# Decode attention with a gated MLP on one core: other places for the rows of wo, and most of w2 loaded in mid-run

## The chip, the core and the metric

The kernel runs on one core of a Trainium2 chip. The metric is the device time of one execution in microseconds (us). The core has a matrix engine (TensorE, PE; its weight loads are PEld), a vector engine (VectorE, DVE), a scalar engine (ScalarE, ACT), GpSimd (POOL) and SyncE (SP), which here only issues transfers. Transfers run on 16 DMA engines, numbered 0 to 15 in this text.

## The reference

One token attends over 32 heads with a cache of 4096 positions each, and the result is mixed with a small MLP of the same token:

```
g = sigmoid(sum(x * gate_w))
q = x @ wq                              # 512 -> 32 heads x 128
p = softmax(q . k_cache / sqrt(128))    # 32 heads x 4096 positions
a = (p @ v_cache) @ wo                  # 32 x 128 -> 512
b = relu(x @ w1 + b1)**2 @ w2 + b2      # 512 -> 1376 -> 512
out = g * a + (1 - g) * b
```

All inputs are bfloat16. K and V are 32 MB each; wq and wo 4 MB each; w1 and w2 1.4 MB each.

## The kernel before

**Heads.** SP loads K and V head by head, 1 MB each, [128 partitions x 8 KB], into eight slots of Kt and eight of Vt; `load_k` and `load_v` wait until a slot is free. V of head h is issued with K of head h + LAG (7). In iteration i of the loop that PE, DVE and ACT each run, half of the scores of head i come from DVE (`ttr`, 16 fused multiply-and-sum instructions, line 636), the other half from PE: `transposes` (line 439) turns K, ACT copies the result out of PSUM, `scores` (line 450) multiplies by q. Maxima are taken for four heads at once (`max_rows`, `max_cols`), ACT makes the exponentials, and `pv` (line 475) multiplies head i - 7 by V, 32 matmuls. `den` and `norm` divide, eight heads at a time.

**wo.** W holds wq (4 MB) first. When q is complete (s_qps reaches 8), the rows of wo for heads 0 to 23 take its place: 96 rows of 32 KB, here called pieces, one to a partition of W. `place` gives the partition of a piece from its kind (INNER, OUTER, SEAM, WRAP) and an engine e; a run (kind, e, k, r, m) is one load of k x m pieces, meant for k DMA engines in a row from engine e on, m pieces each. POOL issues RUNS in the order of the list (line 330); where the next run starts on another engine than the last one ended on, a small load of d rows of w1 into `dm` (line 327) goes ahead, to move POOL's cursor by d engines. SP issues FIRST (line 278), three pieces each, one each in heads HF = 20 onwards, and last the piece REST (line 281). STRIPS lists all of it in order; POOL makes one selection a strip (line 345) for `selA`, the matrix with which `spread_a` (line 507) brings the normed results of heads 0 to 23 to the partitions in which their pieces lie. `out_a` (line 519) multiplies 23 of the 32 columns of W on PE in iterations 34 to 38; DVE does the other nine (`part_y`, lines 683 and 686), and `sum_y` (line 546) adds them in iteration 37. Both wait for all pieces (s_wp, s_wr).

**The MLP.** SP loads w1 at head 8; `mlp_h` (line 493) runs in iteration 24, DVE makes `hs` in iteration 25.

**The tail.** After the last V, when head 24 has left slot 0 of Kt, SP loads w2 in three parts (w2b, the last 96 rows; w2a, ten groups of 128 rows in two halves, split at GS) and the rows of wo for heads 24 to 31 into slot 0 of Kt, in two parts (`wob_sb`, 768 and 256 KB). Then it issues 15 loads of 16 bytes a row, with 1, 2, ... 15 rows (line 301), into a part of w1's tile that nothing reads after; it waits for them at the very end. PE runs `regroup` (lines 525 and 528: transposes the last eight heads and spreads them), then `mlp_out(0)`, `(1)` and `(2)` (line 555, four matmuls a group of rows), then `out_b` (line 537), all into the accumulator `acc`, whose first matmul is the one of `out_a` with start=True. DVE adds b2, PE transposes, DVE copies, SP stores 1 KB (line 303).

Of the kernel before, what the change touches and what calls it, by code (L numbers as in the profile page):

```python
# [5 lines left out]
def bass_gated_mix__gqa_block_cached__dense_activation_squared_relu__decode_kernel(  # L6
# [31 lines left out]
    F = 1376  # L38
    FG = 10
# [13 lines left out]
    LAG = 7  # L53
    NA = 24
    TB = 8
    GS = [0, 5, 10]
    TS = [0, 6, 8]
    TD = 23
    INNER, OUTER, SEAM, WRAP = range(4)
    RUNS = [(INNER, 0, 4, 0, 1), (INNER, 4, 12, 0, 2), (INNER, 4, 12, 1, 2),  # L60
            (OUTER, 4, 3, 0, 1), (SEAM, 7, 2, 0, 1), (OUTER, 9, 7, 0, 1),
            (OUTER, 4, 3, 1, 1), (SEAM, 7, 2, 1, 1), (OUTER, 14, 2, 1, 1),
            (SEAM, 7, 2, 2, 1), (WRAP, 15, 2, 3, 1), (SEAM, 7, 2, 3, 1)]
    FIRST = [(INNER, 0, 3, 1, 1), (INNER, 0, 3, 2, 1), (INNER, 0, 3, 3, 1),
             (OUTER, 0, 3, 0, 1), (OUTER, 0, 3, 1, 1), (OUTER, 0, 3, 2, 1)]
    REST = 126
    HF = 20

    def place(kind, e, k, r, m):
# [16 lines left out]
    def strips():  # L86
        q = 0
        for run in RUNS + FIRST:
            yield (*place(*run), q)
            q += place(*run)[2]  # L90
        yield REST, 1, 1, q

    STRIPS = list(strips())

# [3 lines left out]
    woa_v = A_wo.rearrange("(p t) n -> p (t n)", t=32)  # L98
    wob_v = A_wo[NA * 128:NH * 128, :].rearrange("(p t) n -> p (t n)", t=TB)
    w1_v = B_w1.rearrange("(p t) n -> p t n", t=4)  # L100
    w2_v = B_w2[0:FG * 128, :].rearrange("(p g) n -> p g n", g=FG)

    ctx = ExitStack()
    with ctx:
# [6 lines left out]
        def sem(name):  # L111
            return ctx.enter_context(nc.semaphore(name))
# [3 lines left out]
        W = sb("W", [128, 4 * 4096], bf16)  # L116
# [5 lines left out]
        w1_sb = sb("w1_sb", [128, 4, F], bf16)  # L122
# [121 lines left out]
        s_acc = sem("s_acc")  # L244
        s_fin = sem("s_fin")
        s_out = sem("s_out")
        s_pr = [sem(f"s_pr{n}") for n in range(15)]

        block = ctx.enter_context(nc.Block())

# [1 line left out]
        @block.sync  # L252
        def _(eng):
            for t in range(4):
                eng.dma_start(wq_sb[:, t, :], wq_v[:, t, :]).then_inc(s_wq[t], 16)  # L255

            def load_k(h):
                if h >= NK:
                    eng.wait_ge(s_sd, h - NK + 1)
                    eng.wait_ge(s_t, 2 * (h - NK + 1))  # L260
                eng.dma_start(Kt[:, h % NK, :], k_h[h, :, :]).then_inc(s_k[h % NK], 16)  # L261

            def load_v(h):
                if h >= NV:
                    eng.wait_ge(s_pv, h - NV + 1)
                eng.dma_start(Vt[:, h % NV, :], v_h[h, :, :]).then_inc(s_v[h % NV], 16)  # L266

            for h in range(LAG):
                load_k(h)
            for h in range(NH):  # L270
                load_v(h)
                if h + LAG < NH:
                    load_k(h + LAG)
                if h == HF:
                    eng.wait_ge(s_qps, 8)
                if HF <= h < HF + len(FIRST):
                    p, st, k, q = STRIPS[len(RUNS) + h - HF]
                    eng.dma_start(W[p:p + st * (k - 1) + 1:st, :], woa_v[q:q + k, :],
                                  max_dma_last_dim=8192).then_inc(s_wr, 16)
                if h == HF + len(FIRST):  # L280
                    eng.dma_start(W[REST:REST + 1, :].rearrange("p (s n) -> p s n", s=16),
                                  woa_v[4 * NA - 1:4 * NA, :].rearrange("p (s n) -> p s n", s=16))\
                       .then_inc(s_wr, 16)
                if h == 8:
                    eng.wait_ge(s_z, 1)
                    eng.wait_ge(s_b2, 1)
                    for t in range(4):
                        eng.dma_start(w1_sb[:, t, :], w1_v[:, t, :]).then_inc(s_w1, 16)
            eng.wait_ge(s_sd, NA + 1)
            eng.wait_ge(s_t, 2 * (NA + 1))  # L290
            eng.dma_start(w2b[:, :], B_w2[FG * 128:F, :]).then_inc(s_w2[0], 16)
            for c in range(len(GS) - 1):
                eng.dma_start(w2a[:, GS[c]:GS[c + 1], :], w2_v[:, GS[c]:GS[c + 1], :])\  # L293
                   .then_inc(s_w2[c + 1], 16)
            for c in range(len(TS) - 1):
                eng.dma_start(wob_sb[:, TS[c]:TS[c + 1], :],
                              wob_v[:, TS[c] * DM:TS[c + 1] * DM].rearrange("p (t n) -> p t n", n=DM))\
                   .then_inc(s_wo[c], 16)
            eng.wait_ge(s_sb, 1)
            for n in range(1, 16):  # L300
                eng.dma_start(w1_sb[0:n, 3, 32 * n:32 * n + 8], B_w1[0:n, 0:8]).then_inc(s_pr[n - 1], 16)
            eng.wait_ge(s_f4, 1)
            eng.dma_start(out[0, 0, :].rearrange("(j p) -> j p", p=128), fin4[:, :]).then_inc(s_out, 16)
            eng.wait_ge(s_out, 16)
            for q in s_pr:
                eng.wait_ge(q, 16)


        @block.gpsimd
# [89 lines left out]
        def _(eng):  # L399
# [111 lines left out]
            def out_a(n):  # L511
                if n == 0:
                    eng.wait_ge(s_ac, 2)
                    for q in s_wp:
                        eng.wait_ge(q, 16)
                    eng.wait_ge(s_wr, 16 * (len(FIRST) + 1))
                for t in range(4 * n, min(4 * n + 4, TD)):
                    for j in range(4):
                        eng.matmul(acc[:, j:j + 1], wo_sb[:, t, j * 128:(j + 1) * 128],
                                   o2A[:, t:t + 1], start=(t == 0 and j == 0), stop=False,  # L520
                                   skip_group_check=True)

            def regroup():
                eng.wait_ge(s_on, NH // HPO)
                eng.transpose(KP[0][0:NH - NA, 0:128], onorm[:, NA:NH], ident[:, :]).then_inc(s_oT, 1)
                eng.wait_ge(s_oc, 1)
                for c in range(16):
                    mm = eng.matmul(O2B, selB[:, c // 8, c % 8, :], oB[:, TB * c:TB * c + TB],
                                    start=(c == 0), stop=(c == 15))
                mm.then_inc(s_oT, 1)  # L530
# [17 lines left out]

            def mlp_out(c):
                eng.wait_ge(s_w2[c], 16)  # L550
                for n in [FG] if c == 0 else range(GS[c - 1], GS[c]):
                    M = 128 if n < FG else FR
                    w = w2a[:, n, :] if n < FG else w2b[:, :]
                    for j in range(4):
                        eng.matmul(acc[:, j:j + 1], w[:, j * 128:(j + 1) * 128], hs[0:M, n:n + 1],
                                   start=False, stop=False, skip_group_check=True)

            q_rows(0)
            q_cols(0)
# [3 lines left out]
            for i in range(NH + LAG):  # L563
                if i < NH:
                    transposes(i)
                if 1 <= i <= NH:
                    scores(i - 1)
                if i % 3 == 0 and i // 3 + 1 < 8:
                    q_rows(i // 3 + 1)
                if i % 3 == 2 and i // 3 + 1 < 8:  # L570
                    q_cols(i // 3 + 1)
                if i >= 5 and (i - 5) % 4 == 0 and (i - 5) // 4 < NG:
                    max_rows((i - 5) // 4)
                if i >= 6 and (i - 6) % 4 == 0 and (i - 6) // 4 < NG:
                    max_cols((i - 6) // 4)
                if i == 34:
                    out_a(0)
                if 34 <= i < 39:
                    out_a(i - 33)
                if i >= LAG:  # L580
                    pv(i - LAG)
                if i >= 12 and (i - 12) % HPO == 0:
                    den((i - 12) // HPO)
                if i == 24:
                    mlp_h()
                if i == 32:
                    turn_a()
                if i == 33:
                    spread_a()
                if i == 37:  # L590
                    sum_y()
            regroup()
            eng.wait_ge(s_hs, 2)
            for c in range(len(GS)):
                mlp_out(c)
            for c in range(len(TS) - 1):
                out_b(c)
            eng.wait_ge(s_fin, 1)
# [4 lines left out]
        def _(eng):  # L603
# [85 lines left out]
            for i in range(NH + LAG):  # L689
# [17 lines left out]
                if i == 33:  # L707
                    eng.wait_ge(s_at, 2)
                    eng.tensor_copy(o2A[:, :], O2A).then_inc(s_ac, 1)
                    eng.wait_ge(s_e, NS * 2)  # L710
                    eng.tensor_copy(o2D, O2A[:, TD:32]).then_inc(s_y2, 1)
                    for q in s_wp:
                        eng.wait_ge(q, 16)
                    eng.wait_ge(s_wr, 16 * (len(FIRST) + 1))
                    eng.wait_ge(s_y2, 1)
                    part_y()
            norm(NH // HPO - 1)
# [37 lines left out]
```

## Time and profile before

| | us |
|---|---|
| median of 3 runs | 199.5 (199.47 to 199.66) |
| the profiled execution | 199.27 |
| its span, first to last instruction | 197.5 |

| engine | busy us | share of the span | instructions |
|---|---|---|---|
| PE | 131.7 | 67% | 2399 |
| PEld | 118.4 | 60% | 2405 |
| DVE | 137.9 | 70% | 1151 |
| ACT | 79.5 | 40% | 148 |
| POOL | 27.2 | 14% | 49 |

The DMA engines moved 78.76 MB in 12755 packets. The granted clock of PE was 0.9 of full speed or more in the first 25 us and 0.5 to 0.7 after that.

The page cuts the span into 40 slices of 4.9 us; a digit is the busy share of an engine in tenths (9 is 90% or more). The chain of work that ended last goes back from the last instruction through whatever released each step; its lines give start, length and what. Lines of the timeline give start, length, engine, source line, operation, what it writes and reads, and in brackets the pause before it and what ended the pause. For a transfer, "landing" is the moment when its semaphore gets the count of a DMA engine that has finished its share.

### The profile page before, as it was taken

Reading aid. Unit: us, or ns where it says so; the run is one execution under the profiler, and the core shown is the slowest. Engines: PE = TensorE matmul, PEld = TensorE weight load, DVE = VectorE, ACT = ScalarE, POOL = GpSimd, SP = SyncE. Lnnn points to the kernel's source line nnn. Section 1 sums busy time; section 2 is a strip of 40 time slices with the busy share of each in tenths; the row PEclk is TensorE's granted clock in tenths of the full one; section 3 lists DMA queues with packets and bytes.
Section 4 is the critical chain, followed back from the end, with each engine's and each line's share of the span. In section 5 each row is a group of like instructions: output and inputs, shape, how many; then the busy total and the mean of one; then the engine's idle time right before and its main releaser. Section 6 shows DMA issues by size and latency. Waiting matters only on the chain.

```text
span 197.5 us, 6576 instructions
## 1 busy us (share of the span) xinstructions
PE 131.7 (67%) x2399; PEld 118.4 (60%) x2405; DVE 137.9 (70%) x1151; ACT 79.5 (40%) x148; POOL 27.2 (14%) x49
## 2 busy tenths in 40 slices
PE   0128657499886867816684662568998767785773
PEld 0105637478686667616664662468997667675762
DVE  0307999999998687717867674577769999859010
ACT  2105838466473436503374330633077335430000
POOL 2000000000000000000039800000198630000000
PEclk9999966755555555555576555555555555555555
DMA  6999999999999999999999999999999999999980
GB/s 218 426 430 425 417 418 425 418 422 420 412 415 422 417 423 406 422 418 425 426 403 420 418 415 415 404 415 415 413 418 420 423 413 422 425 402 412 368 312 20
DMA packets 12755, 78.76 MB, mean 399 GB/s; under 512 B 2514, under 2 KB 2612, under 8 KB 3637
## 3 DMA queue, kind: packets, MB, share of 16 engines
q1 hardware_dynamic: 11396, 75.80, 93.4%
q0 software_dynamic: 1312, 2.53, 3.4%
q8 instruction: 19, 0.31, 0.6%
q14 instruction: 14, 0.11, 0.1%
q10 hardware_dynamic: 14, 0.01, 0.0%
HBM read 78.32 MB, written 0.00 MB: 397 GB/s over the span
## 4 chain that ended last, share of the span: by engine, by line
DMA 73%; DVE 12%; SPq 6%; PE 5%; issue 1%; ACT 0%
DMA Kt<-in_A_k_cache_dram 56%; DMA Kt<-in_A_wo_dram 12%; DVE Kt L636 11%; DMA W<-in_A_wq_dram 6%; SPq L266 4%; PE KP L439 2%; PE pQ L417 1%; SPq L261 1%; DVE S L636 1%; SPq L255 1%; PE pX L537 1%; PE pO L475 0%; SPq L293 0%; PE pX L475 0%; PE pS L450 0%
## 5 line engine op out<-in xcount | busy, mean ns | idle before, releaser
L636 DVE CUSTOM_DVE_ANT_0 Kt<-Kt,qb 128x128 bf16<-128x128 bf16 x512 | 112.7, 289 | 24.6 <-DMA Kt<-in_A_k_cache_dram 24.6
L373 ACT ACTIVATE kT<-KP 128x1024 bf16<-128x1024 bf16 x64 | 61.9, 1021 | 68.8 <-PE KP L439 68.8
L439 PE MATMUL KP<-ident,Kt 128*128 128x128 bf16 x512 | 56.1, 297 | 34.0 <-DMA Kt<-in_A_k_cache_dram 34.0
L439 PEld LDWEIGHTS KP<-ident,Kt 128*128 128x128 bf16 x512 | 48.7, 138 | 36.6 <-DMA Kt<-in_A_k_cache_dram 35.5
L636 DVE DVE_READ_ACCUMULATOR2_ANT S<- 128x1 f32 x512 | 41.6, 81 | 0.0
L450 PE MATMUL pS<-qcol,kT 128*128 128x1 bf16 x512 | 19.2, 167 | 8.7 <-DVE S L642 8.5
L450 PEld LDWEIGHTS pS<-qcol,kT 128*128 128x128 bf16 x512 | 18.8, 107 | 10.3 <-DVE S L642 10.2
L330 POOL DMA_DIRECT2D W<-in_A_wo_dram x12 | 7.0, 584 | 100.2 <-PE pQ L417 100.2
L417 PE MATMUL pQ<-W,xb 128*128 128x512 bf16 x26 | 12.3, 617 | 8.1 <-DMA W<-in_A_wq_dram 6.6
L475 PEld LDWEIGHTS pO<-E,Vt 128*128 128x128 bf16 x512 | 15.6, 105 | 1.2 <-issue 0.8
L475 PE MATMUL pO<-E,Vt 128*128 128x1 bf16 x512 | 16.2, 166 | 0.0
L365 ACT ACTIVATE qb<-pQ 128x512 bf16<-128x512 f32 x8 | 4.7, 591 | 15.4 <-PE pQ L417 15.4
L345 POOL TENSOR_SCALAR_AFFINE_SELECT w_sb<-w_sb 24x36 bf16<-24x36 bf16 (+7 forms) x19 | 10.4, 545 | 3.1 <-POOL w_sb L345 0.5
L475 PE MATMUL pQ<-E,Vt 128*128 128x1 bf16 x256 | 8.0, 165 | 4.1 <-DMA Vt<-in_A_v_cache_dram 4.1
L475 PEld LDWEIGHTS pQ<-E,Vt 128*128 128x128 bf16 x256 | 7.7, 104 | 4.4 <-issue 3.1
L417 PEld LDWEIGHTS pQ<-W,xb 128*128 128x128 bf16 x32 | 3.6, 130 | 11.1 <-issue 11.1
L384 ACT ACTIVATE E<-S,nM 128x32 bf16<-128x32 f32 x32 | 9.9, 310 | 0.3
L475 PEld LDWEIGHTS pX<-E,Vt 128*128 128x128 bf16 x256 | 7.8, 104 | 0.7 <-issue 0.6
L475 PE MATMUL pX<-E,Vt 128*128 128x1 bf16 x256 | 8.1, 165 | 0.0
L622 DVE CAST qcol<-pQ 128x4 bf16<-128x4 f32 x8 | 1.2, 153 | 8.7 <-PE pQ L425 8.7
L642 DVE COPY S<-pS 128x16 f32<-128x16 f32 x32 | 5.4, 169 | 2.4 <-PE pS L450 2.4
L645 DVE TENSOR_REDUCE mp<-S 128x1 f32<-128x32 f32 x32 | 6.0, 186 | 1.1
(83 smaller groups left out, 88.4 us busy)
## 6 DMA issues: line engine op xcount, KB each, us to landing
Kt<-in_A_k_cache_dram SPq DMA_DIRECT2D x32, 1024.0 KB, 26.8
Vt<-in_A_v_cache_dram SPq DMA_DIRECT2D x32, 1024.0 KB, 27.5
W<-in_A_wq_dram SPq DMA_DIRECT2D x4, 1024.0 KB, 8.0
W<-in_A_wo_dram POOLq DMA_DIRECT2D x2, 768.0 KB, 13.5
w_sb<-in_B_w_dram SPq DMA_DIRECT2D x4, 344.0 KB, 22.9
w2a<-in_B_w_dram SPq DMA_DIRECT2D x2, 640.0 KB, 21.8
Kt<-in_A_wo_dram SPq DMA_DIRECT2D x1, 768.0 KB, 23.7
W<-in_A_wo_dram SPq DMA_DIRECT2D x6, 96.0 KB
```

The lines of the kernel that those rows point to most:

```text
L266: eng.dma_start(Vt[:, h % NV, :], v_h[h, :, :]).then_inc(s_v[h % NV], 16)
L330: eng.dma_start(W[p:p + st * (k - 1) + 1:st, :], woa_v[q:q + k, :], max_dma_last_dim=8192).then_inc(s_wp[n], 16)
L345: eng.affine_select(out=part, in_=part, compare_op=ALU.not_equal, fill=1.0, base=-st * q, pattern=[[st, 4], [-1, st * (k - 1) + 1]], chann ...
L373: eng.activation(kT[:, h % 2, j * HB * 128:(j + 1) * HB * 128], KP[n % 3][:, :], ACT.Copy).then_inc(s_ev, 1)
L384: eng.activation(E[:, h % NE, :], S[:, h % NS, :], ACT.Exp, bias=nM[:, h:h + 1], scale=SCALE, accum_out=RS[:, h:h + 1]).then_inc(s_e, 1)
L417: mm = eng.matmul(pQ[:, :], xb[:, t, :], wq_sb[:, t, c * 512:(c + 1) * 512], start=(t == 0), stop=(t == 3))
L439: mm = eng.transpose(KP[n % 3][:, y * 128:(y + 1) * 128], Kt[:, h % NK, b * 128:(b + 1) * 128], ident[:, :])
L450: mm = eng.matmul(S2[:, y:y + 1], kT[:, h % 2, y * 128:(y + 1) * 128], qcol[:, h:h + 1], start=True, stop=True)
L475: mm = eng.matmul(O(h, h + 1), Vt[:, h % NV, b * 128:(b + 1) * 128], E[:, h % NE, b:b + 1], start=(b == 0), stop=(b == NB - 1))
L636: ins = eng.tensor_tensor_reduce(kb, kb, qb[:, h * 128:(h + 1) * 128], 1.0, 0.0, ALU.mult, ALU.add, S[:, h % NS, b:b + 1])
L642: eng.tensor_copy(S[:, h % NS, XB:NB], S2).then_inc(s_cp, 1)
L645: eng.tensor_reduce(mp[:, h:h + 1], S[:, h % NS, :], AX.X, ALU.max).then_inc(s_mp, 1)
```

## The change

- RUNS has 13 loads in place of 12, FIRST five in place of six, REST five single pieces (partitions 12, 13, 14, 15 and 44) in place of one (partition 126). REST pieces are issued by SP in heads 20 to 24 beside FIRST, each with a cap of 2048 bytes a descriptor. By the lists, the pieces of engines 0 to 15 without REST go from 8, 7, 7, 1, 6, 6, 6, 8, 8, 5, 5, 5, 5, 5, 6, 7 (95) to 8, 7, 7, 0, 5, 5, 5, 8, 8, 5, 5, 5, 5, 5, 5, 8 (91). The small loads that move POOL's cursor become nine in place of seven, and the selections of line 345 become 23 in place of 19.
- w2a is split 7 to 3. The seven groups are loaded at head 10 and multiplied in iteration 27 (`mlp_out(0)`), which now begins the accumulator; w2b is multiplied inside `regroup`, while PE waits for DVE's copy, and the other three groups after it. In the tail SP loads w2b, the three groups and wo.
- The 15 tiny loads and their semaphores are gone.

```diff
--- before.py
+++ after.py
@@ -53,17 +53,18 @@
     LAG = 7
     NA = 24
     TB = 8
-    GS = [0, 5, 10]
+    GS = [0, 7, 10]
     TS = [0, 6, 8]
     TD = 23
     INNER, OUTER, SEAM, WRAP = range(4)
-    RUNS = [(INNER, 0, 4, 0, 1), (INNER, 4, 12, 0, 2), (INNER, 4, 12, 1, 2),
+    RUNS = [(INNER, 4, 12, 0, 2), (INNER, 4, 12, 1, 2),
             (OUTER, 4, 3, 0, 1), (SEAM, 7, 2, 0, 1), (OUTER, 9, 7, 0, 1),
-            (OUTER, 4, 3, 1, 1), (SEAM, 7, 2, 1, 1), (OUTER, 14, 2, 1, 1),
-            (SEAM, 7, 2, 2, 1), (WRAP, 15, 2, 3, 1), (SEAM, 7, 2, 3, 1)]
-    FIRST = [(INNER, 0, 3, 1, 1), (INNER, 0, 3, 2, 1), (INNER, 0, 3, 3, 1),
-             (OUTER, 0, 3, 0, 1), (OUTER, 0, 3, 1, 1), (OUTER, 0, 3, 2, 1)]
-    REST = 126
+            (SEAM, 7, 2, 1, 1), (WRAP, 15, 2, 1, 1), (OUTER, 1, 2, 1, 1),
+            (SEAM, 7, 2, 2, 1), (WRAP, 15, 2, 2, 1), (OUTER, 1, 2, 2, 1),
+            (SEAM, 7, 2, 3, 1), (WRAP, 15, 2, 3, 1)]
+    FIRST = [(INNER, 0, 3, 0, 1), (INNER, 0, 3, 1, 1), (INNER, 0, 3, 2, 1), (INNER, 0, 3, 3, 1),
+             (OUTER, 0, 3, 0, 1)]
+    REST = [12, 13, 14, 15, 44]
     HF = 20
 
     def place(kind, e, k, r, m):
@@ -88,7 +89,8 @@
         for run in RUNS + FIRST:
             yield (*place(*run), q)
             q += place(*run)[2]
-        yield REST, 1, 1, q
+        for n, p in enumerate(REST):
+            yield p, 1, 1, q + n
 
     STRIPS = list(strips())
 
@@ -244,7 +246,6 @@
         s_acc = sem("s_acc")
         s_fin = sem("s_fin")
         s_out = sem("s_out")
-        s_pr = [sem(f"s_pr{n}") for n in range(15)]
 
         block = ctx.enter_context(nc.Block())
 
@@ -277,33 +278,28 @@
                     p, st, k, q = STRIPS[len(RUNS) + h - HF]
                     eng.dma_start(W[p:p + st * (k - 1) + 1:st, :], woa_v[q:q + k, :],
                                   max_dma_last_dim=8192).then_inc(s_wr, 16)
-                if h == HF + len(FIRST):
-                    eng.dma_start(W[REST:REST + 1, :].rearrange("p (s n) -> p s n", s=16),
-                                  woa_v[4 * NA - 1:4 * NA, :].rearrange("p (s n) -> p s n", s=16))\
-                       .then_inc(s_wr, 16)
+                if HF <= h < HF + len(REST):
+                    p, _, _, q = STRIPS[len(RUNS) + len(FIRST) + h - HF]
+                    eng.dma_start(W[p:p + 1, :], woa_v[q:q + 1, :],
+                                  max_dma_last_dim=2048).then_inc(s_wr, 16)
                 if h == 8:
                     eng.wait_ge(s_z, 1)
                     eng.wait_ge(s_b2, 1)
                     for t in range(4):
                         eng.dma_start(w1_sb[:, t, :], w1_v[:, t, :]).then_inc(s_w1, 16)
+                if h == 10:
+                    eng.dma_start(w2a[:, 0:GS[1], :], w2_v[:, 0:GS[1], :]).then_inc(s_w2[0], 16)
             eng.wait_ge(s_sd, NA + 1)
             eng.wait_ge(s_t, 2 * (NA + 1))
-            eng.dma_start(w2b[:, :], B_w2[FG * 128:F, :]).then_inc(s_w2[0], 16)
-            for c in range(len(GS) - 1):
-                eng.dma_start(w2a[:, GS[c]:GS[c + 1], :], w2_v[:, GS[c]:GS[c + 1], :])\
-                   .then_inc(s_w2[c + 1], 16)
+            eng.dma_start(w2b[:, :], B_w2[FG * 128:F, :]).then_inc(s_w2[1], 16)
+            eng.dma_start(w2a[:, GS[1]:FG, :], w2_v[:, GS[1]:FG, :]).then_inc(s_w2[2], 16)
             for c in range(len(TS) - 1):
                 eng.dma_start(wob_sb[:, TS[c]:TS[c + 1], :],
                               wob_v[:, TS[c] * DM:TS[c + 1] * DM].rearrange("p (t n) -> p t n", n=DM))\
                    .then_inc(s_wo[c], 16)
-            eng.wait_ge(s_sb, 1)
-            for n in range(1, 16):
-                eng.dma_start(w1_sb[0:n, 3, 32 * n:32 * n + 8], B_w1[0:n, 0:8]).then_inc(s_pr[n - 1], 16)
             eng.wait_ge(s_f4, 1)
             eng.dma_start(out[0, 0, :].rearrange("(j p) -> j p", p=128), fin4[:, :]).then_inc(s_out, 16)
             eng.wait_ge(s_out, 16)
-            for q in s_pr:
-                eng.wait_ge(q, 16)
 
 
         @block.gpsimd
@@ -513,16 +509,17 @@
                     eng.wait_ge(s_ac, 2)
                     for q in s_wp:
                         eng.wait_ge(q, 16)
-                    eng.wait_ge(s_wr, 16 * (len(FIRST) + 1))
+                    eng.wait_ge(s_wr, 16 * (len(FIRST) + len(REST)))
                 for t in range(4 * n, min(4 * n + 4, TD)):
                     for j in range(4):
                         eng.matmul(acc[:, j:j + 1], wo_sb[:, t, j * 128:(j + 1) * 128],
-                                   o2A[:, t:t + 1], start=(t == 0 and j == 0), stop=False,
+                                   o2A[:, t:t + 1], start=False, stop=False,
                                    skip_group_check=True)
 
             def regroup():
                 eng.wait_ge(s_on, NH // HPO)
                 eng.transpose(KP[0][0:NH - NA, 0:128], onorm[:, NA:NH], ident[:, :]).then_inc(s_oT, 1)
+                mlp_out(1)
                 eng.wait_ge(s_oc, 1)
                 for c in range(16):
                     mm = eng.matmul(O2B, selB[:, c // 8, c % 8, :], oB[:, TB * c:TB * c + TB],
@@ -548,12 +545,12 @@
 
             def mlp_out(c):
                 eng.wait_ge(s_w2[c], 16)
-                for n in [FG] if c == 0 else range(GS[c - 1], GS[c]):
+                for n in [range(GS[1]), [FG], range(GS[1], FG)][c]:
                     M = 128 if n < FG else FR
                     w = w2a[:, n, :] if n < FG else w2b[:, :]
                     for j in range(4):
                         eng.matmul(acc[:, j:j + 1], w[:, j * 128:(j + 1) * 128], hs[0:M, n:n + 1],
-                                   start=False, stop=False, skip_group_check=True)
+                                   start=(n == 0 and j == 0), stop=False, skip_group_check=True)
 
             q_rows(0)
             q_cols(0)
@@ -583,6 +580,9 @@
                     den((i - 12) // HPO)
                 if i == 24:
                     mlp_h()
+                if i == 27:
+                    eng.wait_ge(s_hs, 2)
+                    mlp_out(0)
                 if i == 32:
                     turn_a()
                 if i == 33:
@@ -590,9 +590,7 @@
                 if i == 37:
                     sum_y()
             regroup()
-            eng.wait_ge(s_hs, 2)
-            for c in range(len(GS)):
-                mlp_out(c)
+            mlp_out(2)
             for c in range(len(TS) - 1):
                 out_b(c)
             eng.wait_ge(s_fin, 1)
@@ -711,7 +709,7 @@
                     eng.tensor_copy(o2D, O2A[:, TD:32]).then_inc(s_y2, 1)
                     for q in s_wp:
                         eng.wait_ge(q, 16)
-                    eng.wait_ge(s_wr, 16 * (len(FIRST) + 1))
+                    eng.wait_ge(s_wr, 16 * (len(FIRST) + len(REST)))
                     eng.wait_ge(s_y2, 1)
                     part_y()
             norm(NH // HPO - 1)
```

## The prediction

> **What bounds the kernel now.** I read the page's time slices first, then the chain of work that ended last, then the DMA view of the last stretch and the timeline of the tail. The page:
>
> ```profile
> span 197.5 us, 6576 instructions
> ...
> PE   0128657499886867816684662568998767785773
> ...
> DMA  6999999999999999999999999999999999999980
> GB/s 218 426 430 425 417 418 425 418 422 420 412 415 422 417 423 406 422 418 425 426 403 420 418 415 415 404 415 415 413 418 420 423 413 422 425 402 412 368 312 20
> ```
>
> Each digit is a fortieth of the span. The DMA engines are full from 5 us on at 402 to 430 GB/s, while PE is full in a few slices alone; only the last three slices (368, 312, 20) fall off. So the time is 78.76 MB at a fixed rate, plus what the tail loses. The chain of the tail:
>
> ```profile
> 169.87 23.75 DMA Kt<-in_A_wo_dram
> 193.62 0.14 issue
> 193.76 1.00 PE pX L537 x32
> 194.76 0.02 issue
> 194.78 0.17 DVE fin L724
> ```
>
> The last transfer (1 MB of wo) lands at 193.62 and 194.24 in its two parts; 32 matmuls, the sum and the store follow. The DMA view of 175 to 197.5 us (slices of 0.56 us) shows how the engines end:
>
> ```profile
> DMA  9999999999999999999999999989742220000000
> ```
>
> From 190.8 us on fewer and fewer engines work (7, 4, 2, 2, 2 tenths). The trace's landing records say which: the 15 tiny loads of line 301 have 1, 2, ... 15 rows, and a load of n rows shows n landings, one an engine, so each load's new first landing tells when one more engine got through its queue. Subtracting the 0.2 us of the tiny load itself and matching with the 16 landings of the last wo part gives the end of each engine (0 to 15): 194.2, 192.6, 191.5, 193.1, 190.0, 194.1, 192.6, 192.2, 191.9, 191.1, 191.2, 191.3, 191.4, 191.7, 194.2, 191.9. Their mean is 191.9; three engines (0, 5, 14) end 2.3 us after it. Everything waits for these.
>
> **The change part by part.**
>
> *Pieces of wo (the term that decides).* A piece is one 32 KB row, four packets of 8 KB; a packet takes 0.309 us when its engine is full, so a piece is 1.24 us. Both versions load 96. By engine, before: 9 on engine 0 (6 from FIRST, 2 from RUNS, and the REST row, which the trace shows as one packet of 32 KB with one landing), 7, 7, 1, 6, 6, 6, 8, 8, then 5 five times, 6, 7. After, without REST: 8, 7, 7, 0, 5, 5, 5, 8, 8, six times 5, 8; that is 91. The five REST rows are cut at 2048 B into 16 descriptors each. The trace has no such load, so both ends: line 281's row ran on one engine, which would put five pieces on engine 0 (+6.2 us there); the loads of line 301 and of the output have the same form (n short descriptors in one count) and ran on n engines, which puts 5/16 = 0.31 piece on each. I take the second, because the form is the same; line 281 was a single descriptor and could not be split. Adding (new minus old pieces) x 1.24 to each engine's end: engine 0 193.3, 1 193.0, 2 191.9, 3 192.2, 4 189.2, 5 193.2, 6 191.7, 7 192.5, 8 192.3, 9 to 13 191.5 to 192.1, 14 193.4, 15 193.5. The last is 193.5 instead of 194.24: 0.7 us. Engine 15 takes the place of 0 and 14.
>
> The Trainium skill, "DMA: Bandwidth & Descriptors", section "Why a DMA increments its semaphore by 16 and not by 1", says a load is split along its slowest dimension that is not of size 1, which agrees with the second end and would keep the sum as it is. The same page, "Latency and other measured facts", calls engines 7 and 15 usually slower than the others, which speaks against giving them 8 pieces; in this trace engine 7 with 8 pieces ended at 192.2, before engine 5 with 6 at 194.1, so I follow the row. The page gives no figure; were engine 15 late by the 1.5 us that engine 5 lies behind engine 6 at equal pieces, it would end at 195.0 and the kernel take 199.9.
>
> *Seven of eleven parts of w2 loaded at h = 10 and multiplied at i = 27.* The bytes are the same (7 x 1 KB a partition, 56 KB an engine, 2.16 us at the packet rate): all K and V behind it arrive 2.16 us later, and the end of the queue stays. The price is cover. Now V31 lands at 188.39, 5.85 us ahead of the last wo; after, only V31's successors w2b, three parts of w2 and wo (94 KB an engine) remain: 3.65 us. The timeline of the tail shows what must fit:
>
> ```profile
> 185.72 0.99 PE L475 MATMUL pQ<-E,Vt 128*128 128x1 bf16 x32 [0.93 <-DMA Vt<-in_A_v_cache_dram]
> 186.57 1.84 PE L546 MATMUL pX<-onesf,kT 128*128 128x1 f32 x8
> 188.28 0.46 PE L519 MATMUL pX<-o2A,W 128*128 128x1 bf16 x12
> 188.60 0.99 PE L475 MATMUL pQ<-E,Vt 128*128 128x1 bf16 x32
> ...
> 190.55 0.58 PE L528 MATMUL pS<-oB,w_sb 8*128 8x8 bf16 x16 [0.31 <-DVE oB L719]
> ...
> 191.17 0.17 DVE L721 CAST o2B<-pS 128x8 bf16<-128x8 f32 x1 [0.68 <-PE pS L528]
> ...
> 192.04 0.99 PE L555 MATMUL pX<-hs,w2a 128*128 128x1 bf16 x32 [0.50 <-issue]
> 193.76 0.99 PE L537 MATMUL pX<-o2B,Kt 128*128 128x1 bf16 x32 [0.72 <-DMA Kt<-in_A_wo_dram]
> ```
>
> From V30's product (185.72) to V31's is 2.88 us without a pause of PE; from there to the end of the regrouping matmuls (line 528) 2.5 us. With the last engine at 193.5, V30 lands 158 KB an engine earlier, 6.1 us: 187.4. Its product starts at 187.5, V31's at 190.4, the regrouping ends at 192.9, twelve w2 matmuls at 27 ns (0.33) follow, then the 32 of wo (1.0): 194.25. On the DMA's side: 193.5 plus the 0.5 that lies between the last landing and the end of line 537 now, 194.0. So PE's route ends 0.2 us after the DMA's and takes part of the gain: 194.75 becomes 194.2 to 194.3, 0.5 us. The four w2b matmuls (0.1) stand before PE's wait for the copy of line 719 and fill the pause of 0.31. The 28 moved matmuls (28 x 27 ns = 0.8 us) fall into iteration 27; the next transposes wait for K anyway:
>
> ```profile
> 153.94 1.89 PE L439 MATMUL KP<-ident,Kt 128*128 128x128 bf16 x16 [1.46 <-DMA Kt<-in_A_k_cache_dram]
> ```
>
> The pause of 1.46 us hides them; without it, the 0.8 us would be caught up by the pauses of 1.4 to 1.6 us before each later head.
>
> *Tiny loads gone.* Engine 0 works through 15 of them until 196.88; the output's four landings are 196.64, 196.67, 196.69 and, on engine 0 behind them, 197.06. After: 196.7. Gain 0.37 us, certain as long as the store ends the kernel. The waits for them end at 196.9, inside the wait for the store: nothing. SP's 10.21 us for issuing them lie after the last real load, with only the output queued behind: nothing.
>
> *Queues.* SP issues one FIRST load fewer, four REST rows more, and w2's main part earlier: net +3 in heads 20 to 24, at 0.74 (line 278) to 2.37 us (line 281) each, 2.2 to 7.1 us of SP; loads land 27 us after their issue, so the engines have that much queued, and it is hidden. If that stock were gone, each microsecond would be a microsecond. POOL issues one load and two dummies more (3 x 0.56 us, at 102 to 114 us; wo is first read at 175.8): nothing. Its selections for selA grow from 19 to 23, 13.1 to 15.9 us, ending near 166 with the later start; spread_a reads them at 175.2: nothing.
>
> **Sum.** 197.47 - 0.5 - 0.37 = 196.6 span; the profiled execution took 199.27 us (1.8 around its span), so 198.4 by its clock. It lies 0.23 under the median 199.5, so I add that: 198.6.
>
> **Rivals.**
>
> - *REST on one engine (slower).* For: line 281's row. Against: its form. Engine 0 would have 13 pieces, 4 more than now: 194.2 + 4.9 = 199.1, everything after it with it, less 0.37: 204 us. It decides as soon as the five rows leave more than 1.3 pieces on engine 0.
> - *An instruction fetch on another engine.* Besides the loads the engines fetch the programs:
>
> ```profile
> q8 instruction: 19, 0.31, 0.6%
> q14 instruction: 14, 0.11, 0.1%
> ```
>
> The packets of queue 8 have 16 KB and hold an engine for about 1.1 us each, and the packet behind them takes half a microsecond more. Taking 1.24 us a piece off the ends above leaves 182 to 184 for engines 0, 1, 2, 4, 7, 8 and 15, some 185 for 6 and 9 to 13, 187 for 5 and 14, 192 for 3: I read that as two fetches on the middle group, three on 5 and 14, and queue 14 on 3. PE's program keeps its length, which speaks for the same places after the change; but one fetch more on engine 0, 14 or 15 makes the last end 195.0: 0.75 after now, less 0.37, 199.9 us.
> - *PE's route.* If PV30, the float32 sums and PV31 meet a later V30 (one more microsecond of skew between engines), line 537 ends where it did: only the 0.37 stays, 199.1.
> - *Better balance than I count.* With the last engine at 192.8 and PE's route 0.5 shorter, because V30 comes from an engine that is late only afterwards: 197.8.
>
> **How the numbers follow.** Forecast 0.62 (its own range 198.1 to 199.0), REST on one engine 0.06, a fetch 0.14, PE's route 0.11, better balance 0.07. A measurement of this kernel tells 0.2% (0.4 us) from no change. Faster: 0.60 of the forecast, the last case, 0.01 of PE's route = 0.68; same: 0.02, 0.10 of PE's route and 0.04 of the fetch = 0.16; slower: the rest, 0.16. The range 197.8 to 200.0 leaves out REST on one engine and the worst of the fetches.
>
> **What would show it.** Last landing of wo near 193.5, with one or two engines, 15 among them, behind the rest, and the DMA digits of the tail falling more steeply; the REST loads each with 16 landings in packets of 2 KB; PE without a pause between line 555 and line 537; the four landings of the output within 0.1 us. Wrong it would be by a last landing at 194 or later, by REST rows landing on one engine, or by pauses of the DMA engines in the middle of the span.

## The result and the profile after

The changed kernel takes 208.02 us (median, 207.69 to 208.06) beside 199.59 us (199.47 to 199.78) of the kernel before: ratio 1.0418, 95% interval 1.0403 to 1.0433. It is 8.4 us slower, where 198.6 us was forecast. Its profiled execution took 207.87 us with a span of 206.1 us. From its page:

```profile
span 206.1 us, 6574 instructions
...
DMA  6999999999999999999999999999999999999100
GB/s 238 425 428 425 418 420 421 415 426 412 421 418 415 423 400 431 409 424 423 413 426 410 420 406 411 417 404 417 407 417 406 407 420 409 420 411 366 64 35 11
```

The slices are 5.15 us here. The body is what it was, 400 to 431 GB/s. The whole loss lies behind 190 us: two slices with 64 and 35 GB/s, little more than one or two engines move (8 KB in 0.309 us is 26 GB/s). The DMA view of 175 to 198 us (0.575 us a digit) shows it more finely:

```profile
DMA  9999999999999999999899999984212011012110
```

Before the change the digits were zero from 193.6 us on. Now they fall earlier, but a tenth or two goes on to the end of the view. The landing records of the last part of wo give the times: 188.85, thirteen between 190.86 and 191.88, then 197.77, then 203.01. The chain of work that ended last, from 160 us on (start, length, what):

```profile
167.34 29.52 DMA Vt<-in_A_v_cache_dram
196.87 0.14 issue
197.00 0.99 PE pQ L471 x32
...
202.42 0.42 PE pX L552 x12
202.83 0.87 PE pX L534 x32
203.71 0.02 issue
```

V30, which V31's product and all after it wait for, lands at 196.87 in place of 187.4, the time the forecast gave it. What the two late engines do follows from the issues of transfers. First the kernel after (destination, source, queue, count, size of each), then before:

```profile
W<-in_A_wo_dram SPq DMA_DIRECT2D x5, 32.0 KB
```

```profile
W<-in_A_wo_dram SPq DMA_DIRECT2D x1, 32.0 KB
```

The five REST rows have one landing each, like the one row before, and the record of each issue names one element of 32768 bytes, as it did for line 281. The packet records show five packets of 32768 bytes, at 145.21, 153.60, 162.11, 170.57 and 178.96 us, 1.88 to 1.99 us each; that they ran on engine 0 is seen in the run of the lists alone, below. The cap of 2048 bytes a descriptor left no trace in the packets. Between two of them lie some 8.4 us, in which engine 0 also moves its parts of K and V (16 packets of 0.309 us, 4.95 us) and one FIRST piece (1.24): a REST row costs 8.4 - 4.95 - 1.24 = 2.2 us. Some 0.3 of it is in the 8 KB packet behind it, which takes 0.61 to 0.63 us in place of 0.31. Four rows more than before put engine 0's end at 194.2 + 4 x 2.2 = 203.0; measured, 203.01.

The other late engine was in no sum. While a REST packet runs, the 8 KB packets of another engine take up to 0.64 us in place of 0.31 (534, 624, 626 and 596 ns one behind the other from 145.67 us on, 1.1 us more than four of 0.31; 1.1 to 1.3 us for each row). The run of the lists alone names it as engine 3, in whose partitions (12 to 15, 44) the REST rows go. Five times some 1.2 us, on the 191.9 us that engine 3 would have without them (193.1 before, less its one piece), gives 197.9; measured, 197.77. The kernel before had it too: its REST row into partition 126, one of engine 15's, took 1920 ns at 172.6 us, and packets of 426, 631, 636 and 611 ns stand beside it.

### The profile page after: what moved, and what is told of

It reads as the page before. It is cut to its first block, busy times and chain, and to the rows that moved or that the text cites. A ratio compares the mean times of both kernels' runs of the same rounds, so it can differ in the third digit from the quotient of the medians.

```text
span 206.1 us, 6574 instructions
## 1 busy us (share of the span) xinstructions
PE 133.4 (65%) x2405; PEld 118.5 (57%) x2405; DVE 138.7 (67%) x1151; ACT 79.6 (39%) x148; POOL 30.6 (15%) x56
## 4 chain that ended last, share of the span: by engine, by line
DMA 75%; DVE 13%; PE 6%; SPq 4%; issue 1%; ACT 0%; DVEq 0%
DMA Kt<-in_A_k_cache_dram 55%; DMA Vt<-in_A_v_cache_dram 14%; DVE Kt L634 11%; DMA W<-in_A_wq_dram 5%; SPq L267 2%; SPq L262 1%; PE KP L435 1%; PE pQ L413 1%; PE pQ L471 1%; PE pX L543 1%; DVE S L634 1%; SPq L256 1%; PE pX L534 0%; PE pO L471 0%; ACT qb L361 0%
## 5 line engine op out<-in xcount | busy, mean ns | idle before, releaser
L323 POOL DMA_DIRECT2D xb<-in_B_w_dram x9 | 5.4, 598 | 102.8 <-PE pQ L413 102.8
L413 PE MATMUL pQ<-W,xb 128*128 128x512 bf16 x32 | 14.9, 621 | 6.3 <-DMA W<-in_A_wq_dram 6.3
L341 POOL TENSOR_SCALAR_AFFINE_SELECT w_sb<-w_sb 24x36 bf16<-24x36 bf16 (+6 forms) x23 | 12.1, 528 | 3.7 <-POOL w_sb L341 0.5
```

The costliest lines, as they stand in the source:

```text
L323: eng.dma_start(dm[0:d, sent, :, 0:8], src[:, :, 0:8]).then_inc(s_dm[sent], 16)
L341: eng.affine_select(out=part, in_=part, compare_op=ALU.not_equal, fill=1.0, base=-st * q, pattern=[[st, 4], [-1, st * (k - 1) + 1]], chann ...
L413: mm = eng.matmul(pQ[:, :], xb[:, t, :], wq_sb[:, t, c * 512:(c + 1) * 512], start=(t == 0), stop=(t == 3))
```

## The experiments

**Each REST row over 16 engines.** The change with the rows as two loads of 16 pieces of 1 KB that do not join up; the partitions stay.

```diff
-                    eng.dma_start(W[p:p + 1, :], woa_v[q:q + 1, :],
-                                  max_dma_last_dim=2048).then_inc(s_wr, 16)
+                    wr = W[p:p + 1, :].rearrange("p (s a n) -> p s a n", s=16, a=2)
+                    ar = woa_v[q:q + 1, :].rearrange("p (s a n) -> p s a n", s=16, a=2)
+                    for a in range(2):
+                        eng.dma_start(wr[:, :, a, :], ar[:, :, a, :]).then_inc(s_wr, 16)
...
```

> The changed kernel with each of the five REST rows loaded as two transfers of 16 separate descriptors of 1 KB, so that all 16 DMA engines carry it; the partitions (12 to 15 and 44) stay. Theory E (a row costs only the engine that carries it): engine 0 loses the five rows, no engine ends after 193.5, and the time is that of the prediction, 198.6 us. Theory P (a row also costs the engine whose partitions it is written to, here engine 3): engine 3 still ends near 197.8 as in the changed kernel, 3.5 us after the last engine of the kernel before, and the time is 199.5 + 3.5 - 0.4 = 202.6 us.

Measured: 202.11 us (201.97 to 202.29), ratio 1.0133 (1.0119 to 1.0147). Its issues of these rows, then its DMA view of 186 to 200 us (0.35 us a digit), then the same view of the changed kernel:

```profile
W<-in_A_wo_dram SPq DMA_DIRECT2D x10, 16.0 KB
```

```profile
DMA  9998979999999989893211000003000000000000
```

```profile
DMA  9998999999898522112100111111311100100000
```

Each of the ten loads now has 16 landings, from 16 elements of 1024 bytes. The last landings of wo are 192.5 to 194.05 and then 197.18 alone. One engine of 16 alone makes a digit of 0 or 1; the 3 near the right is where a 16 KB packet of the instruction queue begins (195.57 us). The spreading takes 5.9 us away, so the five whole rows on engine 0 are the larger part of the loss. One engine is still 3 us behind. That is as it should be if the partitions written into are what makes engine 3 late, since they are the same; the runs with other partitions below test it.

**The lists alone** (RUNS, FIRST, REST and the loads of REST, as in the change) in the kernel before; w2 and the tiny loads stay, and so the tiny loads can name the engines.

```diff
-    REST = 126
+    REST = [12, 13, 14, 15, 44]
...
-        yield REST, 1, 1, q
+        for n, p in enumerate(REST):
+            yield p, 1, 1, q + n
```

> The kernel before with the changed lists of wo rows (RUNS, FIRST, REST) alone; w2 stays in the tail and the 15 tiny loads stay. If the lists are the whole loss: last landing of wo near 203, and with the tiny loads behind it on engine 0 (15 x 0.18 us) the store ends near 206: 207.7 to 208.5 us. If part of the loss comes from the shorter cover in the tail or from w2 in mid-run, this run is faster by that part, 205 us or less.

Measured: 208.46 us (208.37 to 208.58), ratio 1.0451 (1.0435 to 1.0467): the lists are all of the loss. The new first landings of the tiny loads are 203.6 for engine 0, 198.44 for engine 3, 192.69 and 191.44 for engines 1 and 2, and 191.05 and 191.67 for engines 4 and 5: the two late engines are 0 and 3. For engines 4 and 5 these are upper bounds, since both loads landed 0.8 us after the first count on their semaphores (190.26 and 190.88 us), which a load gets when it is issued.

**The old lists** (the same places turned back) in the changed kernel: w2 in mid-run and no tiny loads remain of the change.

```diff
-    REST = [12, 13, 14, 15, 44]
+    REST = 126
...
-        for n, p in enumerate(REST):
-            yield p, 1, 1, q + n
+        yield REST, 1, 1, q
```

> The changed kernel with the lists of wo rows of the kernel before: w2 in mid-run, no tiny loads. If moving w2 costs nothing in mid-run: last landing of wo at 194.2 as before, V30 lands 6.1 us ahead of it (188.1), PE's route ends at 195.0 instead of 194.75, and the store is 0.37 us shorter: 199.4 us, same. If the shorter cover costs a microsecond or more: 200 us or more. If mid-run gains something: under 199.1 us.

Measured: 199.15 us (198.97 to 199.34), ratio 0.9982 (0.9974 to 0.9991).

**The tiny loads alone** taken out of the kernel before.

```diff
-            eng.wait_ge(s_sb, 1)
-            for n in range(1, 16):
-                eng.dma_start(w1_sb[0:n, 3, 32 * n:32 * n + 8], B_w1[0:n, 0:8]).then_inc(s_pr[n - 1], 16)
...
-            for q in s_pr:
-                eng.wait_ge(q, 16)
```

> The kernel before without the 15 tiny loads. If the store waits for them on engine 0: its four landings come within 0.1 us of one another, 0.37 us gained, 199.1 to 199.2 us. If the wait is hidden by the end of the program: 199.5 us.

Measured: 198.97 us (198.65 to 199.02), ratio 0.9971 (0.9961 to 0.9982): 0.55 us off, with 0.36 to 0.78 in the interval; the four landings of the output are 196.70 to 196.76. Beside the run before, w2 in mid-run is worth nothing (199.15 against 198.97). Why is in the waits of PE from 184 to 196 us (what waited, for what, us in total, times, longest), first without w2 in mid-run (this run), then with it (the run before):

```profile
PE pX L531 <- DMA Kt<-in_A_wo_dram: 0.9, 1, 0.9
...
PE pX L549 <- issue: 0.3, 1, 0.3
```

```profile
PE pX L550 <- issue: 0.6, 1, 0.6
```

With w2 in the tail, PE waits for wo for 0.9 us, and a pause of 0.3 that the profile puts down to nothing ("issue") hides in that. With w2 in mid-run the wait for wo is gone and a like pause of 0.6 stands in PE's own chain: the first part of wo landed at 193.34, 0.5 us before its product starts. The timeline of PE in the run with the old lists:

```profile
187.63 0.99 PE L469 MATMUL pQ<-E,Vt 128*128 128x1 bf16 x32
...
190.51 0.99 PE L469 MATMUL pQ<-E,Vt 128*128 128x1 bf16 x32
191.89 0.27 PE L519 MATMUL KP<-ident,onorm 128*8 128x128 bf16 x1 [0.39 <-DVE onorm L659]
192.79 0.25 PE L550 MATMUL pX<-hs,w2b 96*128 96x1 bf16 x4 [0.64 <-issue]
192.97 0.59 PE L523 MATMUL pS<-oB,w_sb 8*128 8x8 bf16 x16
193.49 0.48 PE L550 MATMUL pX<-hs,w2a 128*128 128x1 bf16 x12
193.83 1.00 PE L532 MATMUL pX<-o2B,Kt 128*128 128x1 bf16 x32
```

The product with wo ends at 194.83. Without w2 in mid-run it starts at 193.81 and ends at 194.80.

**Spread and moved**: the first experiment with the rows in five partitions of other engines.

```diff
-    REST = [12, 13, 14, 15, 44]
+    REST = [17, 18, 101, 105, 109]
```

> As the run with the REST rows spread over 16 engines, but the five rows go to free partitions of engines 4 (17, 18), 9 (101), 10 (105) and 11 (109) instead of engine 3's. Theory P (a row costs the engine whose partitions it is written to): engine 3 is no longer late, the receiving engines ended early before and stay under 193, the last engine ends at 193.2 to 193.5, and the time is that of the prediction, 198.6 us. If the loss in the spread run came from the short descriptors or from the ten transfers more in SP's queue: still near 202 us.

Measured: 199.75 us (198.58 to 199.82), ratio 1.0002 (0.9988 to 1.0016). The single engine behind is gone: 192.54 to 193.69, then 194.90 and 195.14. Only the partitions differ from the first experiment, and they are worth some 2.4 us. The 198.6 us expected were not reached: two engines still end 1.2 us behind the others, and what makes them late is taken up below.

**Moved, not spread**: the same line, in the changed kernel itself.

```diff
-    REST = [12, 13, 14, 15, 44]
+    REST = [17, 18, 101, 105, 109]
```

> The changed kernel with the five REST rows in those free partitions, but still one descriptor of 32 KB each on engine 0. Theory P: engine 0 still ends near 203, so the time stays near 208 us; but the engine that was second to last (197.8, taken for engine 3) is gone: all others land wo before 193.5. If the second late engine was late for another reason (instruction fetches): it still lands near 197.8.

Measured: 208.01 us, one execution. Its DMA view of 186 to 200 us:

```profile
DMA  9899999999989974200010000002000000100000
```

All landings but one are at 192.57 or earlier, engine 0's at 203.03. So the second late engine did come from the partitions, and the time stays, since engine 0 alone sets it; the REST packets still take 1.885 to 1.985 us, and packets of up to 0.66 us stand beside them in the new places.

**Other lists**, in the kernel before without tiny loads: pieces of engines 0 to 15 are 8, 7, 7, 0, 5, 5, 5, 8, 8, 6, 6, 6, 6, 5, 4, 8, and two rows are spread over all.

```diff
+    RUNS = [(INNER, 4, 12, 0, 2), (INNER, 4, 12, 1, 2),
+            (OUTER, 4, 3, 0, 1), (SEAM, 7, 2, 0, 1), (OUTER, 9, 5, 0, 1),
+            (SEAM, 7, 2, 1, 1), (OUTER, 9, 4, 1, 1), (WRAP, 15, 2, 0, 1), (OUTER, 1, 2, 0, 1),
+            (SEAM, 7, 2, 2, 1), (WRAP, 15, 2, 1, 1), (OUTER, 1, 2, 1, 1),
+            (SEAM, 7, 2, 3, 1), (WRAP, 15, 2, 2, 1), (OUTER, 1, 2, 2, 1), (WRAP, 15, 2, 3, 1)]
+    FIRST = [(INNER, 0, 3, 0, 1), (INNER, 0, 3, 1, 1), (INNER, 0, 3, 2, 1), (INNER, 0, 3, 3, 1)]
+    REST = [17, 18]
```

> The kernel before without the tiny loads (w2 in the tail) and with lists made from both rules: pieces of engines 0 to 15 are 8, 7, 7, 0, 5, 5, 5, 8, 8, 6, 6, 6, 6, 5, 4, 8, each in its own engine's partitions, and two rows spread over all 16 engines into partitions 17 and 18 of engine 4, which ends earliest. By 1.24 us a piece the last engine ends at 193.05 instead of 194.24: 1.2 us less than the run without tiny loads, 197.8 us. If the fetches of the program move to other engines, or the ends are not additive: 198.5 us or more.

Measured: 198.93 us (197.61 to 199.21), ratio 0.9960 (0.9943 to 0.9978). The executions fall into two groups, four at 197.61 to 198.02 and seven at 198.93 to 199.21. The profiled one (198.93) has two landings at 194.11 and 194.25, the others by 192.83.

**The same lists with w2 in mid-run**: RUNS, FIRST and the spread loads of REST as above, in the changed kernel.

```diff
-    REST = [12, 13, 14, 15, 44]
+    REST = [17, 18]
```

> The same lists with w2's seven groups in mid-run as in the change. If the shorter cover binds, PE's route (V30, the float32 sums, V31, regrouping, wo) ends 0.3 to 0.6 us after what the last landing alone would give, and this run is 0.2 to 0.5 us slower than the one with w2 in the tail: 198.1 us. If the cover is enough: equal to it, 197.8 us.

Measured: 198.74 us (198.60 to 199.19), ratio 0.9964 (0.9950 to 0.9977). Both forecasts were missed, by 0.6 and 0.9 us. In its profiled execution (199.19) all of wo has landed at 193.15, 1.1 us before the run above, and nothing is won. From PE's timeline:

```profile
185.80 0.81 PE L472 MATMUL pQ<-E,Vt 128*128 128x1 bf16 x25 [1.59 <-issue]
...
190.20 0.99 PE L472 MATMUL pQ<-E,Vt 128*128 128x1 bf16 x32
192.58 0.27 PE L522 MATMUL KP<-ident,onorm 128*8 128x128 bf16 x1 [1.39 <-issue]
...
194.00 1.00 PE L535 MATMUL pX<-o2B,Kt 128*128 128x1 bf16 x32
```

After V31's product PE stands still for 1.39 us ahead of the regrouping, and wo's product starts at 194.00. The two pauses end 1.42 and 1.56 us after the end of a 16 KB packet of the instruction queue (183.22 to 184.38 and 190.00 to 191.02 us).

**The other lists with the tiny loads kept**, so that these name the engines, and later the same kernel again.

```diff
+            eng.wait_ge(s_sb, 1)
+            for n in range(1, 16):
+                eng.dma_start(w1_sb[0:n, 3, 32 * n:32 * n + 8], B_w1[0:n, 0:8]).then_inc(s_pr[n - 1], 16)
...
```

> The first of the two kernels with new lists (w2 in the tail), with the 15 tiny loads put back behind wo, so that the end of every engine shows. Its trace without them had two engines at 194.1 and 194.25, the rest under 192.9. If the late pair is where the fetches of the program fall a third time, the late engines are two of 9 to 12 (two fetches and six pieces: 192.6; three: 194.1) and 5 and 14 are not late. If the late ones are 0 or 15 (eight pieces), the price of a piece is wrong. Time 0.4 us over the run without them.

Measured: 197.93 us (two executions, 197.80 and 198.07), ratio 0.9922 (0.9904 to 0.9940); landings of wo 191.6 to 193.14, no late engine.

> The kernel with new lists and tiny loads again, in more executions, since two gave 197.8 and 198.1 and the same lists without tiny loads gave two groups of times (197.6 to 198.0, 198.9 to 199.2). If the groups come from where the late instruction fetches fall in an execution: both groups show up here too, and a profile of the slower group has one or two of the engines with fetches (5, 6, 9 to 14) about 1.4 us behind the rest, while one of the faster group has none. If the groups come from the tiny loads being gone: all executions lie at 197.6 to 198.2.

Measured: 198.10 us (197.77 to 199.18), ratio 0.9948 (0.9927 to 0.9968), with 197.77, 198.04, 198.06 and 198.13 in one group and 198.93 and 199.18 in the other. So the groups do not come from the tiny loads being gone. The profiled execution (197.77) is of the faster one; its DMA view of 186 to 200 us, and below the same view of the lists without tiny loads (198.93):

```profile
DMA  9999999899999988720000000000000000000000
```

```profile
DMA  8999999999989896521311000000000000000000
```

The slower group's profile has two engines that end 1.3 us later; which they are was not seen, but the records show when they fell behind. The landings of V29 end at 181.53 and 181.54, those of V30 at 184.00 and then 185.51, and in between lies a 16 KB packet of the instruction queue (181.60 to 182.71 us). The second engine falls behind between the two halves of w2a (188.75, then 191.62 or 191.75), where the next such packet lies (189.41 to 190.49). In the faster profile the packets come at nearly the same times (181.33 and 188.13 us), and no engine falls behind the rest. So the two groups fit the engine on which an instruction packet falls: in the slower one it was twice one that was among the last already. The two late engines of the run with the rows spread and moved fall behind at such packets too (183.70 and 190.27 us).

By its median this kernel is the fastest of all here, 1.4 to 1.5 us under the kernel before and 10 us under the change; but the median depends on how many executions fall into each group (six of eight in the faster one here, four of eleven without the tiny loads).

**The change's lists, rows spread and moved** (each as two loads of 16 x 1 KB), first in the kernel before without tiny loads, then in the changed kernel.

```diff
-    REST = [12, 13, 14, 15, 44]
+    REST = [11, 12, 17, 18, 19]
```

> The changed kernel's RUNS and FIRST (eight pieces for the engines that hardly get fetches, five for the nine that do), no tiny loads, w2 in the tail, and the five REST rows spread over 16 engines into partitions 11 (engine 2), 12 (engine 3) and 17 to 19 (engine 4). With three fetches a five-piece engine ends at 193.2, an eight-piece engine without one at 193.2: last landing 193.2 to 193.5 whichever engine the fetches fall on, 197.9 us with little spread. If the fetch places matter more than that: two values more than 1 us apart, as with the first new lists.

Measured: 198.79 us (198.62 to 199.05), ratio 0.9966 (0.9953 to 0.9978); three landings at 194.20 to 194.24, one at 193.87. There is one group of times, as expected, but it lies 0.9 us above the forecast.

> The changed kernel whole (w2 in mid-run), with only the REST rows mended: spread over 16 engines, and into the same partitions 11, 12, 17, 18, 19. By the terms of the prediction 198.6 us; if the shorter cover costs what the two runs with the first new lists or the two with the old lists showed (0.2 us), 0.2 us over the run with w2 in the tail.

Measured: 199.08 us (198.69 to 199.46), ratio 0.9981 (0.9972 to 0.9989); last landing 194.41. This is the change as described, with the REST rows alone put right (spread, and in other partitions): 0.4 us faster than before, not 8.4 slower. With the rows in the other free partitions (17, 18, 101, 105 and 109, above) it was 199.75 us.

## Why the prediction was wrong

**The step that failed** is the one on the REST rows: "I take the second, because the form is the same; line 281 was a single descriptor and could not be split." The two ends were the right ones, and the choice between them was wrong. Line 281 is written as 16 pieces of a row and yet was one packet of 32 KB: pieces that lie end to end on both sides were joined, as now those under the cap. The loads of line 301 have n rows in n partitions, which cannot join. The nearest row of the trace was the contiguous one, and it had already shown what would happen. The Trainium skill ("DMA: Bandwidth & Descriptors", "Why a DMA increments its semaphore by 16 and not by 1") splits by the slowest dimension not of size 1 as the instruction carries it, and names [1, 1] as one engine. The runs agree: the issue record has [1,1] elements of 32768 bytes and the row one landing; 16 pieces that cannot join have [16,1] elements of 1024 bytes and 16 landings. I had applied the rule to the source text.

**The rival's price was short.** The rival "REST on one engine" had chance 0.06 and 204 us. Its mechanism is what happened, down to engine 0; its term, four rows at 1.24 us, measured 2.2 each, since one packet of 32 KB takes 1.9 us where four of 8 KB take 1.24, and the packet behind it takes 0.3 us more. The difference, 4 x 0.96 = 3.8 us, is nearly all of the way from its last landing at 199.1 to 203.0.

**A term was missing.** A row written into another engine's partitions costs that engine 1 us or more. With the rows spread it is worth 2.4 us (202.11 against 199.75); in the change itself engine 0 ends later still, and it costs nothing (208.01 against 208.02).

**The other pieces.** With REST put right, the last landing is 194.2 to 194.4, not 193.5. The engines do end closer together: the last landing lies 1.0 to 1.3 us behind the mean of the 16, where it was 2.1 before. But the mean itself is later. It is 192.18 us before, 192.21 in the change with its two late engines, 192.26 to 192.34 in the profiles with two spread rows and 193.06 to 193.27 in the four with five. So spreading five rows goes with 0.9 to 1.1 us more on the mean, where the forecast left it in place; what takes that time was not separated. Eight pieces on an engine are not the reason by themselves: with 8 on engines 0, 7, 8 and 15 the last landing was 193.10 to 193.15 in three profiles.

The ends that the balance was built on were themselves set by instruction packets, as far as the times show. In the kernel before, single engines fall behind three times: by 1.5 us with the landings that end at 177.78 us, a second one with those that end at 185.58, and a third between 190.21 and 191.75. A 16 KB packet of the instruction queue lies ahead of each (175.13 to 176.23, 181.68 to 182.88 and 189.52 to 190.55 us). That makes three late engines, as many as the prediction found (0, 5 and 14), in the way its rival of the fetches describes. Moving pieces does not keep such a packet from falling on another late engine. This rests on times that agree; no run here moved the packets on purpose. The 191.9 us that the prediction calls the mean of the ends is their middle value; the mean is 192.2, and no term rests on it.

The same skill page's remark that engines 7 and 15 are usually slower ("Latency and other measured facts") has no support here: before, engine 7 ended at 192.2 with 8 pieces and engine 15 at 191.9 with 7, both no later than the mean.

**w2 in mid-run.** The 28 matmuls hide, as said; the pause for K stays, 1.06 us long (the run with the old lists):

```profile
153.70 0.89 PE L550 MATMUL pX<-hs,w2a 128*128 128x1 bf16 x28
155.64 1.89 PE L433 MATMUL KP<-ident,Kt 128*128 128x128 bf16 x16 [1.06 <-DMA Kt<-in_A_k_cache_dram]
```

The route of PE in the changed kernel itself, to be held against the predicted parts:

```profile
197.00 0.99 PE L471 MATMUL pQ<-E,Vt 128*128 128x1 bf16 x32 [0.56 <-DMA Vt<-in_A_v_cache_dram]
...
199.88 0.99 PE L471 MATMUL pQ<-E,Vt 128*128 128x1 bf16 x32
...
201.84 0.58 PE L525 MATMUL pS<-oB,w_sb 8*128 8x8 bf16 x16
202.35 0.48 PE L552 MATMUL pX<-hs,w2a 128*128 128x1 bf16 x12
202.69 1.00 PE L534 MATMUL pX<-o2B,Kt 128*128 128x1 bf16 x32
```

From V30's product to V31's it is 2.88 us, from there to the end of line 525 2.54: right, to 0.04. With V30 in time, the second part has a pause of 0.64 (old lists) or 1.39 us (other lists) that the forecast did not have, and none with the change's lists put right. In three pairs w2 in mid-run cost 0.2 and 0.3 us and gained 0.2 us (199.15 and 198.97; 199.08 and 198.79; 198.74 and 198.93), and the intervals of each pair overlap; the last pair compares with a run of two groups. Two profiles with the same end of wo say more: with w2 in mid-run the last landing at 193.15 gave 199.19 us, with w2 in the tail and the tiny loads kept the one at 193.10 gave 197.77. So once wo lands early, PE's route decides, as the rival on PE's route said, though its reason was another: the pauses. In nine of the traces PE has such pauses after 184 us, 14 of 0.19 to 1.59 us, and each ends 1.2 to 1.6 us after the end of a 16 KB packet of the instruction queue. Between one such pause and the next PE has exactly 256 instructions on record, in all seven pairs counted in five of the traces. So PE most likely waits there for the next block of its own program; that is read from these times and counts, and no run tests it.

**The tiny loads.** 0.37 us was predicted, 0.55 measured, with 0.37 inside the interval; the output's landings lie within 0.06 us of each other, as said. **Queues**: POOL's last selection starts at 163.8 us, and `spread_a` reads them at 187.7; right.

## What to carry to other kernels

How many engines a transfer uses is to be read from its landings, its packet sizes and the elements in its issue record, not from the shape it is written in: pieces that lie end to end become one descriptor. Where the trace of before holds the very load that is multiplied, its row outweighs a load that only looks alike. Before loads are balanced over engines, count also what is written into an engine's partitions from elsewhere, and look whether the compute behind the last landing leaves room for a gain.

## What the runs showed of the hardware

- A packet of 32 KB takes 1.88 to 1.99 us, and the 8 KB packet behind it 0.61 to 0.63 in place of 0.31 us; four of 8 KB take 1.24 us.
- A write of a 32 KB row into partitions that another engine is filling takes that engine's 8 KB packets from 0.31 to as much as 0.66 us while it lasts, some 1.2 us a row, in all three sets of partitions (126; 12 to 15 and 44; 17, 18, 101, 105 and 109). A row cut up and sent by all 16 engines still cost the partitions' engine about 1 us, an estimate from the first experiment: (197.18 - 191.9 - 0.4 for its own share of the five rows) / 5.
- The same program with the same loads ran in two groups 1.0 us apart (197.6 to 198.1 and 198.9 to 199.2). In the profile of the slower group two engines fall behind at the times of two 16 KB instruction packets, each about 1.1 us long; in that of the faster group none does.
- Pauses of PE that the profile puts down to "issue" (14 after 184 us, in nine traces) all end 1.2 to 1.6 us after the end of a 16 KB instruction packet, and neighbouring ones lie 256 PE instructions apart (seven pairs in five traces).
